# Attention and a feed-forward block on one Trainium2 core: GpSimd's shifted additions as 64-bit integer adds with the addend in the instruction

## The chip, the cores and the metric

The kernel runs on one core of a Trainium2 chip. The metric is the device time of one execution in microseconds. Beside TensorE (PE in the profile, its weight loads PEld) a core has VectorE (DVE), ScalarE (ACT), GpSimd (POOL) and SyncE (SP, which here issues DMAs). All have queues of their own and wait for each other by semaphores.

## The reference

A layer norm of x, attention with 32 heads of size 20 that share one key and one value head, and a feed-forward block with silu, all added up; 2048 positions of width 640:

```python
x = A_x
xn = _layernorm(x, axis=-1)
# A: q = xn @ wq (32 heads), k = xn @ wk, v = xn @ wv (one head)
scores = jnp.einsum("bhqd,bkd->bhqk", q, k) * (Dh ** -0.5)
p = _softmax(scores, axis=-1)
o = jnp.einsum("bhqk,bkd->bhqd", p, v)
# B: h = silu(xn @ w1); out = h @ w2
return x + o_merged @ wo + B
```

## The kernel before

The scores are made transposed: a block is 128 keys by 512 queries of one head. There are 2048 blocks (32 heads, 4 chunks of queries, 16 tiles of keys), in 32 groups of 64 (four heads of one chunk). PE makes the scores of a block in a bank of PSUM (the matmuls of L1122). From there a block goes one of two ways.

- On ACT, `exp` (L1156), two or three blocks in an instruction, into the ring `E`.
- On VectorE, without an exponential: the score is scaled so that its value, clamped and written as a 16-bit integer (L1171, into `Z`), has the bits of a bfloat16 that approximates the exponential. One such reading is coarse. Two more readings of the same numbers, shifted by 43 and by 86 (`PH`), are written into `Y`, and the three are multiplied with three differently scaled copies of v and added up by PE.

These shifted additions are the work that the change touches. `flush_z` is called when up to three blocks (`ZB`) have been gathered in one of four sets (`NZ`) of `Z` and `Y`. It makes two additions for each set. The second always goes to GpSimd (L1208); the first goes to GpSimd or VectorE (L1202), whichever the planner thinks will be free earlier. On GpSimd the 16-bit numbers are taken in pairs as 32-bit integers, and what is added is a tensor: one word for each partition, with the constant twice in it (`cy`, set at L1594), broadcast along the row.

PE then multiplies the readings with v (the PV matmuls, L962), adding up a whole group in one bank. At a group's end VectorE copies the bank out (L1252), a DMA transposes it, VectorE takes the reciprocal of the sums (L1236), and GpSimd multiplies (L1241, a tensor_tensor, `normalise`; the last group does this on VectorE). So GpSimd's queue has, in each group, about a dozen additions and one multiplication. At the start it also does a part of the layer norm, and makes the second copy of the keys (L1805, a tensor_scalar), of which VectorE's blocks have need.

The projections, the feed-forward block and the output's matmuls (most of L861) are filled in between by PE; VectorE and ACT take their results out.

The order of everything is set before the run by a planner (`Sched`): each operation has a supposed duration, the planner plays the engines through, and what it commits is the order of each engine's queue, with semaphore waits for each dependence. For an addition on GpSimd it reckons `YP_FIX + YP_BLK * n`, that is 0.15 + 0.426 n us for n blocks. An operation with `lock` isn't planned beside a locked one of the other of VectorE and GpSimd, and a GpSimd operation also waits for the last VectorE addition planned before it. In the run no queue changes its order.

Of the kernel before, what the change touches and what calls it, by code (L numbers as in the profile page):

```python
# [9 lines left out]
F32 = mybir.dt.float32  # L10
I16 = mybir.dt.int16
I32 = mybir.dt.int32
AF = mybir.ActivationFunctionType
ALU = mybir.AluOpType

# [33 lines left out]
PH = ((0, 1.0), (43, 0.8046875), (86, 0.625))  # L49
# [387 lines left out]
def t_dve_4x(n):  # L437
    return n / 3840.0 + 0.065
# [10 lines left out]
def t_act(n):  # L449
    return n / 1200.0 + 0.0635  # L450
# [27 lines left out]
class Builder:  # L478
# [16 lines left out]
    def sb(self, shape, dt):  # L495
        self.nsb += 1
        return self.stack.enter_context(self.nc.sbuf_tensor(f"sbt{self.nsb}", shape, dt))

    def alloc(self):
# [40 lines left out]
        self.eps = sb([P, 1], F32)  # L540
        self.cy = sb([P, 2], I32)
        self.zero = sb([P, 512], BF16)
# [526 lines left out]
    def do_S(self, now):  # L1069
# [76 lines left out]
        for run in runs:  # L1146
# [7 lines left out]
            def efn(a, run=run, na=na, b0=b0, step=step):  # L1154
                src = self.ps[:, :].rearrange("p (b n) -> p b n", n=BANK)[:, run[0]:run[-1] + 1:step, :]
                return a.activation(self.E[:, b0 * QW:(b0 + na) * QW].rearrange("p (b n) -> p b n", n=QW), src, AF.Exp,  # L1156
                                    scale=ACT_SCALE)
# [29 lines left out]
    def flush_z(self):  # L1187
        sc = self.sc
        zs = self.zset
        n = len(self.zblocks)  # L1190
        self.zset = (self.zset + 1) % NZ
        zk = [("Z", zs, i) for i in range(n)]
        w = n * QW
        back = {e: max(sc.t[e], sc.t["pe"]) + sum(o.dur for o in sc.pend[e]) for e in ("dve", "pool")}
        tp = YP_FIX + YP_BLK * n
        td = Y_SLOW + t_dve_4x(w)
        y0 = "pool" if back["pool"] + tp * Y0_COST < back["dve"] + td + Y0_POOL else "dve"
        self.y0_pool += y0 == "pool"
        for k, e in ((0, y0), (1, "pool")):
            yk = [("Y", zs, k, i) for i in range(n)]  # L1200
            if e == "dve":
                sc.new("dve", td, lambda v, k=k: v.tensor_scalar(  # L1202
                    self.Y[:, zs, k, 0:w], self.Z[:, zs, 0:w], float(PH[k + 1][0]), None, ALU.add), zk, yk,
                    prio=4.0, name=f"y{k}").lock = True
                continue
            c = self.cy[:, k:k + 1]
            cb = bass.AP(self.cy, c.offset, [list(c.ap[0]), [0, w // 2]])
            sc.new("pool", tp, lambda v, k=k, cb=cb: v.tensor_tensor(  # L1208
                self.Y[:, zs, k, 0:w].bitcast(I32), self.Z[:, zs, 0:w].bitcast(I32), cb, ALU.add), zk + [("cy",)], yk,
                prio=4.0, name=f"yp{k}").lock = True  # L1210
        for i, (t, g, kt, j) in enumerate(self.zblocks):
            for k in range(2):
                self.item(g, j, kt, k + 1, lambda k=k, i=i: self.Y[:, zs, k, i * QW:(i + 1) * QW].bitcast(BF16),
                          [("Y", zs, k, i)])
            self.g_late[g] -= 1
        self.zblocks = []
# [50 lines left out]
    def q_job(self, ht, act=False, lo=0, hi=QW):  # L1267
# [7 lines left out]
        def consume(b):  # L1275
# [3 lines left out]
            if act:  # L1279
                sc.new("act", t_act(hi - lo), lambda a: a.activation(dst, self.bk(b, 0, hi - lo), AF.Identity, bias=self.offq[:, :],  # L1280
                                                                scale=C1), [("B", b), ("offq",)], ks, prio=2.0,
# [42 lines left out]
    def h_job(self, c, fk, step):  # L1324
# [17 lines left out]
        def consume(b):  # L1342
            tp = fk % 2
            t = self.tb[0:rows, tp, :]
            src = self.bk(b, 0, QW, 0, rows)
            sc.new("act", t_act(QW), lambda a: a.activation(t, src, AF.Tanh, scale=0.5), [("B", b)], [("tb", tp)],  # L1346
                   prio=TH_PRIO, name=f"th{c}_{fk}").late = 0.06
# [40 lines left out]
    def out_job(self, c, i, e, step=-1, ffn=True, ks=range(DC), src="xres", dst="ost", use=None):  # L1388
# [18 lines left out]
        def consume(b):  # L1407
# [22 lines left out]
            if src == "ps":  # L1430
                sc.new("act", t_act(320), lambda a: a.activation(ost[:, e0:e0 + 320], ps, AF.Copy, scale=0.5),  # L1431
                       [("B", b)], wk, prio=X_PRIO, name=f"out{n}_{e}")
# [93 lines left out]
    def prologue(self):  # L1526
# [92 lines left out]
        def wkrep(a):  # L1619
            dst = self.wk[:, :, :].rearrange("p c (r j) -> p c r j", j=SLOT)[:, :, :, 0:DH]  # L1620
            s = self.kv_st[:, 0, :, :]
            src = bass.AP(self.U, s.offset, [list(s.ap[0]), list(s.ap[1]), [0, 4], [1, DH]])
            return a.activation(dst, src, AF.Copy)
        np_("act", t_act(400), wkrep, [("st", "k")], [("wk",)], prio=1.0, name="wkrep")
        for kk in range(2):
            np_("act", t_act(400), lambda a, kk=kk: a.activation(wqd[:, :, 4 * kk:4 * kk + 4, 0:DH],
                                                                 wqs[:, :, 4 * kk:4 * kk + 4, :], AF.Copy),
                [("wqd", kk)], [("wq", kk)], prio=1.0 + 5 * kk, name=f"wq{kk}")
# [28 lines left out]
        def mvk(a, b_):  # L1657
            return [("mv", n) for n in range(a, b_)]
# [30 lines left out]
        def newton(a, b_, pr, eng):  # L1689
# [5 lines left out]
            def nw(fn, r, w):  # L1695
                ch.append(np_(eng, 0.09, fn, r, w, prio=pr, name="nw"))
                ch[-1].lock = True
                self.last_nw = ch[-1]
                if len(ch) > 1:
                    ch[-2].then = ch[-1]  # L1700
            nw(lambda v: v.tensor_scalar(v_, self.mv[:, a:b_, 1], EPS, None, ALU.add), mvk(a, b_), [("va", a)])
            nw(lambda v: v.tensor_scalar(y_.bitcast(I32), v_.bitcast(I32), -0.5, 1597463007.0, ALU.mult, ALU.add),
               [("va", a)], [("rs", a)])
# [199 lines left out]
```

## Time and profile before

| | before |
|---|---|
| median of 3 runs | 672.74 us (672.58 to 672.9) |
| the profiled execution | 672.72 us |
| its span, first to last instruction | 670.8 us |
| busy: PE, ACT, DVE, POOL | 662.6, 657.7, 621.4, 570.3 us |
| additions on GpSimd (L1208) | 373, 529.9 us busy |
| additions on VectorE (L1202) | 107, 61.5 us busy |
| GpSimd's multiplications (L1241) | 31, 22.6 us busy |

The times come from one profiled execution, beside which the others were measured without a profile. A line of a view names the source line, the engine, the operation, and what it writes and reads (partitions x elements and type). "Idle before, releaser" is how long the engine had nothing to do in front of these instructions, and what ended that. PE's ends are modelled; the other engines' are seen.

### The profile page before, as it was taken

Reading aid. Unit: us, or ns where it says so; the run is one execution under the profiler, and the core shown is the slowest. Engines: PE = TensorE matmul, PEld = TensorE weight load, DVE = VectorE, ACT = ScalarE, POOL = GpSimd, SP = SyncE. Lnnn points to the kernel's source line nnn. Section 1 sums busy time; section 2 is a strip of 40 time slices with the busy share of each in tenths; the row PEclk is TensorE's granted clock in tenths of the full one; section 3 lists DMA queues with packets and bytes.
Section 4 is the critical chain, followed back from the end, with each engine's and each line's share of the span. In section 5 each row is a group of like instructions: output and inputs, shape, how many; then the busy total and the mean of one; then the engine's idle time right before and its main releaser. Section 6 shows DMA issues by size and latency. Waiting matters only on the chain.

```text
span 670.8 us, 22772 instructions
## 1 busy us (share of the span) xinstructions
PE 662.6 (99%) x9713; PEld 223.7 (33%) x9715; DVE 621.4 (93%) x1099; ACT 657.7 (98%) x730; POOL 570.3 (85%) x475
## 2 busy tenths in 40 slices
PE   8999999999999999999999999999999999999998
PEld 4422223333333233333333333332222333333224
DVE  7889999998999998999999999999999999999995
ACT  7999999999999999999999999999999999999995
POOL 6799987598989997789989888878989888888783
PEclk9999999999999999999999999999999999999999
DMA  7568000000013100010003210000000320000101
GB/s 209 96 229 251 25 15 12 10 10 18 10 23 103 29 10 18 10 11 17 18 1 50 84 30 11 10 10 18 17 10 10 79 66 10 11 17 11 33 9 41
DMA packets 51385, 27.72 MB, mean 41 GB/s; under 512 B 37238, under 2 KB 50646, under 8 KB 51286
## 3 DMA queue, kind: packets, MB, share of 16 engines
q1 hardware_dynamic: 49830, 26.05, 14.6%
q8 instruction: 78, 1.28, 0.8%
q10 hardware_dynamic: 1456, 0.22, 0.2%
q14 instruction: 21, 0.17, 0.1%
HBM read 11.44 MB, written 2.62 MB: 21 GB/s over the span
## 4 chain that ended last, share of the span: by engine, by line
PE 85%; ACT 8%; DVE 3%; POOL 2%; DMA 1%; SPq 1%; issue 0%; DVEq 0%; POOLq 0%
PE psall L962 30%; PE psall L1122 28%; PE psall L861 26%; ACT sbt L1156 8%; DVE sbt L1171 1%; DVE sbt L1682 1%; DVE sbt L1652 1%; DMA sbt<-in_A_x_dram 1%; SPq L1542 0%; POOL sbt L1208 0%; POOL sbt L1678 0%; DMA sbt<-sbt 0%; PE psall L1336 0%; POOL sbt L1805 0%; PE psall L828 0%
## 5 line engine op out<-in xcount | busy, mean ns | idle before, releaser
L1156 ACT ACTIVATE sbt<-psall 128x1024 bf16<-128x1024 f32 (+1 forms) x638 | 624.7, 1133 | 2.1 <-PE psall L1122 1.5
L1208 POOL TENSOR_TENSOR sbt<-sbt 128x768 int32<-128x768 int32 (+1 forms) x373 | 529.9, 1449 | 75.9 <-DVE sbt L1202 58.1
L1171 DVE TENSOR_SCALAR sbt<-psall 128x512 int16<-128x512 f32 x707 | 463.5, 685 | 34.0 <-PE psall L1122 23.0
L962 PE MATMUL psall<-sbt 128*32 128x512 bf16 x3462 | 265.4, 383 | 0.0
L1122 PE MATMUL psall<-sbt 32*128 32x512 bf16 x2048 | 248.9, 384 | 1.7 <-DVE sbt L1422 0.5
L861 PE MATMUL psall<-sbt 128*32 128x320 bf16 (+2 forms) x3939 | 225.9, 331 | 0.4 <-DVE sbt L1654 0.3
L1122 PEld LDWEIGHTS psall<-sbt 32*128 32x128 bf16 x2048 | 64.3, 91 | 241.4 <-issue 87.0
L861 PEld LDWEIGHTS psall<-sbt 128*32 128x32 bf16 x3939 | 83.8, 95 | 87.1 <-issue 53.7
L962 PEld LDWEIGHTS psall<-sbt 128*32 128x32 bf16 x3462 | 65.4, 95 | 98.3 <-issue 70.0
L1202 DVE TENSOR_SCALAR sbt<-sbt 128x1536 int16<-128x1536 int16 (+2 forms) x107 | 61.5, 588 | 0.1
L1351 DVE SCALAR_TENSOR_TENSOR sbt<-sbt,psall 128x512 bf16<-128x512 bf16 x54 | 36.7, 679 | 0.8 <-ACT sbt L1346 0.5
L1346 ACT ACTIVATE sbt<-psall 128x512 bf16<-128x512 f32 x54 | 36.2, 670 | 0.0
L1241 POOL TENSOR_TENSOR sbt<-sbt 128x320 bf16<-128x320 bf16 x31 | 22.6, 729 | 4.3 <-DVE sbt L1202 3.4
L1252 DVE CAST sbt<-psall 128x512 bf16<-128x512 f32 x32 | 21.8, 682 | 2.6 <-PE psall L962 2.4
L1415 DVE SCALAR_TENSOR_TENSOR sbt<-psall,sbt 128x320 bf16<-128x320 f32 x28 | 13.6, 484 | 0.9 <-PE psall L861 0.7
L1434 DVE SCALAR_TENSOR_TENSOR sbt<-psall,sbt 128x320 bf16<-128x320 f32 x28 | 13.2, 482 | 1.0 <-PE psall L861 1.0
L1303 DVE TENSOR_SCALAR sbt<-psall 128x512 bf16<-128x512 f32 (+1 forms) x19 | 13.0, 683 | 1.1 <-PE psall L861 1.0
L837 PE MATMUL psall<-sbt 128*128 128x512 bf16 (+3 forms) x43 | 11.9, 424 | 1.3 <-DVE sbt L1591 1.2
L1652 DVE BATCH_NORM_STATS2 sbt<-sbt 128x6 f32<-128x320 bf16 x20 | 9.0, 472 | 3.2 <-DMA sbt<-in_A_x_dram 3.0
L1236 DVE RECIPROCAL sbt<-sbt 128x16 f32<-128x16 bf16 x31 | 7.6, 244 | 0.0
L837 PEld LDWEIGHTS psall<-sbt 128*128 128x128 bf16 x45 | 4.6, 107 | 6.6 <-issue 2.4
L1431 ACT ACTIVATE sbt<-psall 128x320 bf16<-128x320 f32 x4 | 1.6, 438 | 4.3 <-PE psall L861 4.2
(70 smaller groups left out, 93.8 us busy)
## 6 DMA issues: line engine op xcount, KB each, us to landing
sbt<-in_A_x_dram SPq DMA_DIRECT2D x32, 160.0 KB, 3.5
out_dram<-sbt SPq DMA_DIRECT2D x15, 160.0 KB, 2.0
sbt<-in_B_w_dram SPq DMA_DIRECT2D x5, 432.0 KB, 6.0
sbt<-sbt SPq DMA_DIRECT2D x105, 20.0 KB
sbt<-in_B_w_dram SPq DMA_DIRECT2D x13, 160.0 KB, 3.0
sbt<-sbt SPq DMA_DIRECT2D x1, 1024.0 KB, 6.1
sbt<-sbt SPq DMA_TRANSPOSE x56, 2.4
sbt<-in_A_wo_dram SPq DMA_DIRECT2D x5, 160.0 KB, 2.8
```

Of the source, the lines that this page charges most:

```text
L837: return pe.matmul(self.bk(b, 0, n), self.zero[:, 0:P], self.zero[:, 0:n], start=True, stop=True)
L861: ins = pe.matmul(self.bk(b, 0, n, r, r + SLOT), w[:, r:r + SLOT], x, start=start, stop=stop, tile_position=(0, r), skip_group_check=True)
L962: ins = pe.matmul(self.bk(ub[k], 0, QW, r, r + SLOT), self.v[:, it.w, it.kt, :], it.x(), start=f, stop=False, tile_position=(0, r), skip_g ...
L1122: ins = pe.matmul(self.bk(bank[x]), self.kT[r:r + SLOT, kk, kt * P:(kt + 1) * P], self.qT[r:r + SLOT, g % 8, (g // 8) % 2, :], start=True, ...
L1156: return a.activation(self.E[:, b0 * QW:(b0 + na) * QW].rearrange("p (b n) -> p b n", n=QW), src, AF.Exp, scale=ACT_SCALE)
L1171: return v.tensor_scalar(self.Z[:, zs, zp * QW:(zp + 1) * QW], self.bk(bb), 0.0, ZMAX, ALU.max, ALU.min)
L1202: sc.new("dve", td, lambda v, k=k: v.tensor_scalar(self.Y[:, zs, k, 0:w], self.Z[:, zs, 0:w], float(PH[k + 1][0]), None, ALU.add), zk, yk, ...
L1208: sc.new("pool", tp, lambda v, k=k, cb=cb: v.tensor_tensor(self.Y[:, zs, k, 0:w].bitcast(I32), self.Z[:, zs, 0:w].bitcast(I32), cb, ALU.ad ...
L1241: op = sc.new(eng, 0.69 if eng == "pool" else t_dve_ps(16 * DH), lambda v: v.tensor_tensor(dst, ut[:, :, :, 0:DH], rb, ALU.mult), [key, (" ...
L1252: sc.new("dve", t_dve_ps(QW), lambda v: v.tensor_copy(self.U[:, up, :], self.bk(ub)), [("B", ub)], [("U", up)], prio=U_PRIO, name=f"Uev{g}")
L1346: sc.new("act", t_act(QW), lambda a: a.activation(t, src, AF.Tanh, scale=0.5), [("B", b)], [("tb", tp)], prio=TH_PRIO, name=f"th{c}_{fk}") ...
L1351: sc.new("dve", t_dve_ps(QW), lambda v: v.scalar_tensor_tensor(out=self.hT[0:rows, fk, :], in0=t, scalar=1.0, in1=src, op0=ALU.add, op1=AL ...
```

## The change

The GpSimd additions are issued as `int64_add` in place of `tensor_tensor`. The same 16-bit numbers are taken four at a time as one 64-bit integer, and the addend is a number in the instruction (the constant four times), not a tensor. No sum goes over 16 bits, so nothing is carried from one number into the next. The planner's durations and all dependences stay (that on `cy` too, though it isn't read any more), so each queue has its operations in the same order as before.

```diff
+I64 = mybir.dt.int64
...
-            c = self.cy[:, k:k + 1]
-            cb = bass.AP(self.cy, c.offset, [list(c.ap[0]), [0, w // 2]])
-            sc.new("pool", tp, lambda v, k=k, cb=cb: v.tensor_tensor(
-                self.Y[:, zs, k, 0:w].bitcast(I32), self.Z[:, zs, 0:w].bitcast(I32), cb, ALU.add), zk + [("cy",)], yk,
+            c = PH[k + 1][0] * (1 + (1 << 16) + (1 << 32) + (1 << 48))
+            sc.new("pool", tp, lambda v, k=k, c=c: v.int64_add(
+                self.Y[:, zs, k, 0:w].bitcast(I64), self.Z[:, zs, 0:w].bitcast(I64), c), zk + [("cy",)], yk,
                 prio=4.0, name=f"yp{k}").lock = True
```

`int64_add` is an instruction of the program builder's own: `out = in0 + in1` over 64-bit words, exact. The builder has a table of which set of GpSimd code holds which instruction. Its stock set lists tensor_tensor, tensor_scalar and others; the sets that list `int64_add` list neither of these two.

## The prediction

> **What bounds the kernel now.** I read the page's head and chain first, then the busy times by stretch, the groups by form, the waits, and GpSimd's own timeline.
>
> ```profile
> span 670.8 us, 22772 instructions
> PE 662.6 (99%) x9713; PEld 223.7 (33%) x9715; DVE 621.4 (93%) x1099; ACT 657.7 (98%) x730; POOL 570.3 (85%) x475
> PE 85%; ACT 8%; DVE 3%; POOL 2%; DMA 1%; SPq 1%; issue 0%; DVEq 0%; POOLq 0%
> L1156 ACT ACTIVATE sbt<-psall 128x1024 bf16<-128x1024 f32 (+1 forms) x638 | 624.7, 1133 | 2.1 <-PE psall L1122 1.5
> ```
>
> Two engines are full, PE (its ends are modelled) and ACT (its ends are seen). ACT runs the exponentials of L1156 and waited only 2.1 us in front of all 638 of them. GpSimd is the one engine with air, 15%, and has 2% of the chain. The stretch that carries the attention, from the first normalisation to the last, says it more sharply:
>
> ```profile
> core 0: us, PE busy (x) PEld busy (x) DVE busy (x) ACT busy (x) POOL busy (x), PEclk, DMA share, GB/s
> 58.30:653.00 594.70, 593.39 (x8832) 194.12 (x8820) 560.93 (x956) 593.87 (x645) 517.31 (x381) 1.00 0.11 28
> ```
>
> ACT is busy for 593.87 of 594.70 us, so GpSimd's speed as such is worth almost nothing here. POOL is idle for 594.70 - 517.31 = 77.4 us. Who waits for whom:
>
> ```profile
> POOL sbt L1208 <- DVE sbt L1202: 58.1, 72, 2.1
> POOL sbt L1208 <- DVE sbt L1171: 17.0, 19, 1.8
> PEld psall L962 <- POOL sbt L1208: 5.5, 24, 0.3
> DVE sbt L1171 <- POOL sbt L1208: 0.7, 3, 0.2
> ```
>
> The adds of L1208 wait for VectorE, for 75 us in all, and are waited for by the PV matmuls of L962, 24 times, at most 0.3 us each. PE runs a fixed order, so these 24 places say that the plan brings many shifted readings only just in time. A late add stops PE at once, and with PE, soon after, ACT.
>
> **The change, the add itself.** 373 adds change form. What they cost now, and the nearest one-input rows:
>
> ```profile
> L1208 POOL TENSOR_TENSOR sbt<-sbt 128x768 int32<-128x768 int32 x360 | 517.8, 1467 | 71.7 <-DVE sbt L1202 54.0 <-DVE sbt L1171 17.0
> L1208 POOL TENSOR_TENSOR sbt<-sbt 128x256 int32<-128x256 int32 x2 | 1.2, 612 | 0.8 <-DVE sbt L1202 0.8
> L1678 POOL TENSOR_SCALAR sbt<-sbt 128x640 bf16<-128x640 bf16 x3 | 2.6, 879 | 0.0
> L1805 POOL TENSOR_SCALAR sbt<-sbt 128x256 bf16<-128x256 bf16 x8 | 3.8, 482 | 0.5 <-DVE sbt L1803 0.5
> L1241 POOL TENSOR_TENSOR sbt<-sbt 128x320 bf16<-128x320 bf16 x31 | 22.6, 729 | 4.3 <-DVE sbt L1202 3.4 <-DVE sbt L1236 0.9
> ```
>
> With two inputs an element costs (1467 - 612) / 512 = 1.67 ns. With one input it costs (879 - 482) / 384 = 1.03 ns over a fixed 217 ns. The new add has one input, since the addend is in the instruction. Of 1536 readings it makes 384 words of 64 bits: if each is one step, 217 + 384 x 1.03 = 614 ns; if each goes as two 32-bit halves, 217 + 768 x 1.03 = 1011 ns. I take the middle, 0.81 us, and keep 0.61 and, as if nothing were won, 1.47 as ends. At 0.81 an add saves 0.66 us, and all of them 373 x 0.66 = 246 us of GpSimd's time. By the waits above that buys PE 5.5 us of waits at the most, and the end only what ACT lost, 2.1 us.
>
> **The change, what has to be loaded.** No row shows this; it is read from the program's text. The 64-bit add isn't one of GpSimd's stock instructions. The builder's table puts it into a set of GpSimd code that is loaded at run time and that holds neither the tensor_tensor of L1241 nor the tensor_scalar of L1805, and the stock set doesn't hold the 64-bit add. Where the resident set may lack an instruction, the builder puts a load in front of it, on GpSimd's own queue. Today's adds share a set with L1241 and L1805; after the change each alternation is a load. How often they alternate:
>
> ```profile
> 27.28 1.47 POOL L1208 TENSOR_TENSOR sbt<-sbt 128x768 int32<-128x768 int32 x1
> 28.73 0.48 POOL L1805 TENSOR_SCALAR sbt<-sbt 128x256 bf16<-128x256 bf16 x1
> 29.17 1.47 POOL L1208 TENSOR_TENSOR sbt<-sbt 128x768 int32<-128x768 int32 x1
> 30.62 0.94 POOL L1805 TENSOR_SCALAR sbt<-sbt 128x256 bf16<-128x256 bf16 x2
> 31.52 1.47 POOL L1208 TENSOR_TENSOR sbt<-sbt 128x768 int32<-128x768 int32 x1
> 32.96 0.48 POOL L1805 TENSOR_SCALAR sbt<-sbt 128x256 bf16<-128x256 bf16 x1
> 33.41 1.47 POOL L1208 TENSOR_TENSOR sbt<-sbt 128x768 int32<-128x768 int32 x1
> 35.42 0.48 POOL L1805 TENSOR_SCALAR sbt<-sbt 128x256 bf16<-128x256 bf16 x1 [0.54 <-DVE sbt L1803]
> 35.87 12.85 POOL L1208 TENSOR_TENSOR sbt<-sbt 128x768 int32<-128x768 int32 x9
> 48.66 0.63 POOL L1765 MEMSET sbt<- 128x640 bf16 x1
> 49.79 8.58 POOL L1208 TENSOR_TENSOR sbt<-sbt 128x768 int32<-128x768 int32 x6 [0.50 <-DVE sbt L1202]
> 58.33 0.73 POOL L1241 TENSOR_TENSOR sbt<-sbt 128x320 bf16<-128x320 bf16 x1
> ```
>
> Up to 58.33 us that is one load ahead of the first add and two for each of four excursions to L1805: 9 (a plain memset needs no set). After that L1241 comes 31 times, each time with adds before and behind it, the last time too:
>
> ```profile
> L1241 POOL TENSOR_TENSOR sbt<-sbt x31: 724/729/734, 58.3 to 653.0; 128x320 bf16<-128x320 bf16 x31
> L1208 POOL TENSOR_TENSOR sbt<-sbt x373: 612/1466/1475, 27.3 to 660.3; 128x768 int32<-128x768 int32 x180, 128x512 int32<-128x512 int32 x5, 128x256 int32<-128x256 int32 x2
> ```
>
> So 62 more, 71 in all. A last one that restores the stock set comes after 661 us and has about 9 us to the end of the span: I cost it at nothing; with that cover gone it is one load.
>
> The price of a load isn't in the trace. The nearest rows are a table load on ACT and transfers by size:
>
> ```profile
> L1727 ACT ACT_TABLE_LOAD x1 | 1.3, 1283 | 1.8 <-issue 1.8
> ```
> ```profile
> sbt<-in_B_w_dram SPq DMA_DIRECT2D x5, 432.0 KB, 6.0
> sbt<-in_B_w_dram SPq DMA_DIRECT2D x13, 160.0 KB, 3.0
> sbt<-sbt SPq DMA_DIRECT2D x1, 1024.0 KB, 6.1
> ```
>
> Code for eight cores is nearer to a large transfer than to one table, and GpSimd must come to rest and start again around it, about the 0.50 us that a hand-over takes it at 49.79. I take 6.1 + 0.5 = 6.6 us. The ends are 1.3 (the table) and 12 (two transfers of 6.0, if fetching and first use come one after the other). The Trainium skill's GPSIMD Engine Reference, Instruction dispatch, says that the first call of a freshly loaded kernel also pays an instruction-memory load of about 6 us (5.95 measured), not visible as an instruction; by that figure alone the sum below would be 984 us, and no run here has shown it yet.
>
> **The sum.** The start, 27.28 to 58.33: 9 x 6.6 = 59.4 us of loads; 19 adds save 12.5, and 0.54 + 0.50 us of idle time can go: 45.9 us late. The adds and the key copies there feed PE directly, so this is all lost. The main stretch: around each L1241 GpSimd stands still for 2 x 6.6 = 13.2 us more than now. Against that it has its idle time, 77.4 / 31 = 2.5 us per normalisation, and 0.66 us from the faster first add: 10.04 us late, for the first add behind it. The adds after that run faster than PE asks for them (11.4 per normalisation, 9.2 us of work in about 20), so the delay comes once per normalisation: 31 x 10.04 = 311.2 us. Queued behind a load are the adds; PE waits for these, and ACT and VectorE for PE's scores. The lateness doesn't carry over, because the next normalisation is put off with the rest.
>
> The profiled execution took 672.72 us, 1.92 more than its span, and stands 0.02 below the median of the runs. 672.72 + 45.9 + 311.2 = 1029.8, say 1030 us. The add's own ends move this little: at 0.61 us it is 10 less; at 1.47, 33 more.
>
> **Rivals.**
>
> *PE runs at half speed after each standstill (1083 us, 25%).* The kernel's first matmuls, which wait for nothing, show such a phase:
>
> ```profile
> core 0: us, PE busy (x) PEld busy (x), PEclk, DMA share, GB/s
> 1.10:4.50 3.40, 3.31 (x8) 1.16 (x9) 1.00 0.79 178
> 4.50:9.20 4.70, 4.70 (x22) 2.11 (x21) 1.00 0.98 297
> ```
>
> Eight in 3.40 us, then 22 in 4.70: 425 ns each against 214, while the granted clock reads 1.00 in both. Half of 3.40 us is lost, 1.7; if each of 31 standstills of 10 us brings it back, 31 x 1.7 = 53 us more. Against it: ACT sets the pace, and PE has waits to give up. The Trainium skill's TensorE: Matmul & The Clock Gate, Part 1, has this rule: idle for about 3.4 us, half the clock until about 3.4 us of work; the start agrees, and before this change no later stretch can show it.
>
> *GpSimd only has to be fast enough on average (836 us, 10%).* If lateness is absorbed by the four sets of buffers, only GpSimd's own work counts: 71 x 6.6 + 373 x 0.81 + 31 x 0.73 + 6 x 0.48 + 0.63 = 797 us from 27.3 on, 9.4 us of tail and the 1.92. For it: four sets exist. Against it: PE already waits 24 times.
>
> *Loads at other prices.* At 3.0 us (the 160 KB row) 31 x (6.0 - 3.16) + 27 - 13.5 = 101 us are added: 774 us, 6%. At 12 us, 31 x 20.84 + 94.5 = 740: 1413 us, 5%.
>
> *Faster (670.6 us, 3%), or no change (6%).* If the code is resident after all, or a load is short, only the lighter add is left. The place is the idle time around L1241: two loads fit into 2.5 + 0.66 = 3.16 us, so the point is 1.58 us a load (at the start 13.5 / 9 = 1.5). Below that, PE's 5.5 us of waits go and ACT gets at most its 2.1 us back. The table load's 1.3 us speaks for it, the transfer rows against it.
>
> **How the numbers follow.** The forecast itself has 45%: 1030 us. Left out of the range are the cheap loads, the very dear ones, and the two cases of no loss, 20% together. 830 takes in the absorbed case. Loads of 9 us make 672.72 + 31 x 14.84 + 67.5 = 1200, and with the slow phase 1253: the upper end is 1250. Slower: 45 + 25 + 10 + 6 + 5 = 91%. About 0.2%, 1.35 us, is what can be told from no change here; within it 6%, faster 3%.
>
> **What would show it.** Right: adds of about 0.8 us; in front of each L1241 and of the first add behind it, 6 to 7 us in which GpSimd does nothing that VectorE explains, 62 times; L962's waits for L1208 up from 5.5 to about 300 us; ACT with as much idle time, busy about 64%; a first such pause before 30 us. The slow phase would show as eight or so matmuls at twice their spacing behind each pause. Wrong: no pauses, or pauses only once; adds over 1.5 us; ACT still full.

## The result and the profile after

| | before | after |
|---|---|---|
| median of 3 runs | 672.74 us | 1091.01 us (1086.82 to 1097.08) |
| ratio | 1 | 1.6227, 95% interval 1.6104 to 1.635 |
| the profiled execution, its span | 672.72, 670.8 us | 1086.82, 1084.9 us |
| additions on GpSimd, mean of one | 1449 ns | 813 ns |

The additions became 44% shorter, and the kernel takes 62% longer. The page's head, its row of granted clocks and its chain, after:

```profile
span 1084.9 us, 22914 instructions
PE 738.9 (68%) x9713; PEld 230.2 (21%) x9715; DVE 623.8 (57%) x1099; ACT 671.5 (62%) x730; POOL 341.7 (31%) x475
PEclk8755888788789888878888879888888888888888
PE 58%; issue 26%; DVE 8%; POOL 6%; ACT 2%; DMA 0%; DVEq 0%; POOLq 0%
```

No engine is full any more, and 26% of the chain is "issue", time in which an engine waited for nothing that the profile shows. The groups and the waits name the engine:

```profile
L1157 ACT ACTIVATE sbt<-psall 128x1024 bf16<-128x1024 f32 (+1 forms) x638 | 637.0, 1096 | 394.6 <-PE psall L1123 393.3
L1208 POOL INT64_ADD sbt<-sbt x373 | 299.6, 813 | 461.6 <-issue 208.2
L1241 POOL TENSOR_TENSOR sbt<-sbt 128x320 bf16<-128x320 bf16 x31 | 22.2, 717 | 220.3 <-issue 112.8
```
```profile
ACT sbt L1157 <- PE psall L1123: 393.3, 111, 15.2
PE psall L963 <- POOL sbt L1208: 305.2, 40, 13.5
POOL sbt L1208 <- issue: 208.2, 35, 6.3
POOL sbt L1241 <- issue: 112.8, 16, 7.8
POOL sbt L1241 <- DVE sbt L1172: 100.5, 14, 7.7
```

ACT waits for PE's scores, PE for GpSimd's additions (305.2 us; before only its weight loads did, 5.5 us), and GpSimd, ahead of these, for nothing. "Issue" means 208.2 / 35 = 5.95 us in front of an addition and 112.8 / 16 = 7.05 in front of a normalisation. Of the other pauses in front of L1241, 14 are put down to VectorE's L1172; they are as long (100.5 / 14 = 7.2), so the name only says which semaphore came last. GpSimd's timeline shows both kinds (start, duration, instruction, pause ahead of it):

```profile
8.99 0.28 POOL L1587 TENSOR_SCALAR_AFFINE_SELECT sbt<-sbt 128x128 f32<-128x128 f32 x1 [8.00 <-issue]
...
41.22 0.82 POOL L1208 INT64_ADD sbt<-sbt  x1 [5.95 <-issue]
51.25 0.47 POOL L1805 TENSOR_SCALAR sbt<-sbt 128x256 bf16<-128x256 bf16 x1 [9.22 <-issue]
57.64 0.82 POOL L1208 INT64_ADD sbt<-sbt  x1 [5.92 <-issue]
...
127.22 0.72 POOL L1241 TENSOR_TENSOR sbt<-sbt 128x320 bf16<-128x320 bf16 x1 [7.83 <-issue]
133.82 2.42 POOL L1208 INT64_ADD sbt<-sbt  x3 [5.89 <-issue]
...
1061.23 0.72 POOL L1241 TENSOR_TENSOR sbt<-sbt 128x320 bf16<-128x320 bf16 x1 [6.78 <-issue]
1067.77 2.42 POOL L1208 INT64_ADD sbt<-sbt  x3 [5.82 <-issue]
```

In GpSimd's queue each of these pauses begins with a pair of short instructions that the views by line count (least, median and largest duration in ns, then the first and the last start; the row of the additions is shown with them):

```profile
L1241 POOLq MODIFY_POOL_CONFIG  x62: 10/11/13, 119.4 to 1054.5; - x62
...
L1208 POOL INT64_ADD sbt<-sbt x373: 387/824/829, 41.2 to 1072.9; - x187
L1208 POOLq MODIFY_POOL_CONFIG  x72: 1/1/11, 35.5 to 1062.2; - x72
...
L1805 POOLq MODIFY_POOL_CONFIG  x8: 1/1/1, 42.1 to 87.6; - x8
...
L1587 POOLq MODIFY_POOL_CONFIG  x2: 11/11/11, 1.1 to 1.2; - x2
```

Ahead of L1241, L1208 and L1805 that makes 31, 36 and 4 pairs: 71 loads. One more pair stands ahead of L1587, the program's first stock instruction. The kernel before has that pair too, at the same place, and there the pause is 0.17 us:

```profile
L1587 POOLq MODIFY_POOL_CONFIG  x2: 11/11/11, 1.1 to 1.1; - x2
...
1.18 0.29 POOL L1587 TENSOR_SCALAR_AFFINE_SELECT sbt<-sbt 128x128 f32<-128x128 f32 x1 [0.17 <-POOL sbt L1594]
```

So a pair alone doesn't stop the engine; what the 8.00 us of the changed kernel hang on is shown by the last experiments. Over the 31 normalisations the pause ahead of L1241 is 7.10 us in the mean (6.73 to 7.83), and that ahead of the first addition behind it 5.94 (5.76 to 6.28).

The 414.1 us by which the span grew lie in three places. The first L1241 moved from 58.33 to 127.22 us: 68.9 more. From there to the last one it was 594.7 us and is 934.0: 339.3 more, 11.3 for each of 30 intervals. Behind the last it was 17.8 us and is 23.7: 5.9 more, the load ahead of 1067.77.

### The profile page after: what moved, and what is told of

Its sections match the earlier page's. It is cut to its first block, busy times and chain, and to the rows that moved or that the text cites. A ratio compares the mean times of both kernels' runs of the same rounds, so it can differ in the third digit from the quotient of the medians.

```text
span 1084.9 us, 22914 instructions
## 1 busy us (share of the span) xinstructions
PE 738.9 (68%) x9713; PEld 230.2 (21%) x9715; DVE 623.8 (57%) x1099; ACT 671.5 (62%) x730; POOL 341.7 (31%) x475
## 2 busy tenths in 40 slices
DMA packets 51386, 27.73 MB, mean 26 GB/s; under 512 B 37238, under 2 KB 50646, under 8 KB 51286
## 4 chain that ended last, share of the span: by engine, by line
PE 58%; issue 26%; DVE 8%; POOL 6%; ACT 2%; DMA 0%; DVEq 0%; POOLq 0%
PE psall L963 21%; PE psall L1123 18%; PE psall L862 17%; DVE sbt L1172 6%; POOL sbt L1208 3%; POOL sbt L1241 2%; ACT sbt L1157 2%; DVE sbt L1203 0%; PE psall L1795 0%; DVE sbt L1303 0%; PE psall L1776 0%; DMA sbt<-sbt 0%; DVE sbt L1351 0%; PE psall L1336 0%; PE psall L1815 0%
## 5 line engine op out<-in xcount | busy, mean ns | idle before, releaser
L1157 ACT ACTIVATE sbt<-psall 128x1024 bf16<-128x1024 f32 (+1 forms) x638 | 637.0, 1096 | 394.6 <-PE psall L1123 393.3
L1172 DVE TENSOR_SCALAR sbt<-psall 128x512 int16<-128x512 f32 x707 | 467.1, 685 | 428.5 <-PE psall L1123 388.8
L963 PE MATMUL psall<-sbt 128*32 128x512 bf16 x3462 | 309.2, 433 | 305.2 <-POOL sbt L1208 305.2
L1208 POOL INT64_ADD sbt<-sbt x373 | 299.6, 813 | 461.6 <-issue 208.2
L1123 PE MATMUL psall<-sbt 32*128 32x512 bf16 x2048 | 269.5, 418 | 24.7 <-POOL sbt L1805 12.3
L862 PE MATMUL psall<-sbt 128*32 128x320 bf16 (+2 forms) x3939 | 236.2, 343 | 0.1
L963 PEld LDWEIGHTS psall<-sbt 128*32 128x32 bf16 x3462 | 68.7, 98 | 430.1 <-POOL sbt L1208 329.3
L862 PEld LDWEIGHTS psall<-sbt 128*32 128x32 bf16 x3939 | 86.3, 98 | 95.7 <-issue 63.2
L1241 POOL TENSOR_TENSOR sbt<-sbt 128x320 bf16<-128x320 bf16 x31 | 22.2, 717 | 220.3 <-issue 112.8
L1203 DVE TENSOR_SCALAR sbt<-sbt 128x1536 int16<-128x1536 int16 (+2 forms) x107 | 56.9, 545 | 0.1
L1415 DVE SCALAR_TENSOR_TENSOR sbt<-psall,sbt 128x320 bf16<-128x320 f32 x28 | 13.5, 484 | 1.2 <-PE psall L862 1.0
L1434 DVE SCALAR_TENSOR_TENSOR sbt<-psall,sbt 128x320 bf16<-128x320 f32 x28 | 13.2, 482 | 1.4 <-PE psall L862 1.4
L1805 POOL TENSOR_SCALAR sbt<-sbt 128x256 bf16<-128x256 bf16 x8 | 3.8, 470 | 30.6 <-issue 30.6
L1776 PE MATMUL psall<-sbt 128*128 128x128 bf16 x35 | 4.0, 260 | 7.8 <-DVE sbt L1682 7.7
```

The source lines that it names most:

```text
L862: ins = pe.matmul(self.bk(b, 0, n, r, r + SLOT), w[:, r:r + SLOT], x, start=start, stop=stop, tile_position=(0, r), skip_group_check=True)
L963: ins = pe.matmul(self.bk(ub[k], 0, QW, r, r + SLOT), self.v[:, it.w, it.kt, :], it.x(), start=f, stop=False, tile_position=(0, r), skip_g ...
L1123: ins = pe.matmul(self.bk(bank[x]), self.kT[r:r + SLOT, kk, kt * P:(kt + 1) * P], self.qT[r:r + SLOT, g % 8, (g // 8) % 2, :], start=True, ...
L1172: return v.tensor_scalar(self.Z[:, zs, zp * QW:(zp + 1) * QW], self.bk(bb), 0.0, ZMAX, ALU.max, ALU.min)
L1203: sc.new("dve", td, lambda v, k=k: v.tensor_scalar(self.Y[:, zs, k, 0:w], self.Z[:, zs, 0:w], float(PH[k + 1][0]), None, ALU.add), zk, yk, ...
L1208: sc.new("pool", tp, lambda v, k=k, c=c: v.int64_add(self.Y[:, zs, k, 0:w].bitcast(I64), self.Z[:, zs, 0:w].bitcast(I64), c), zk + [("cy", ...
```

## The experiments

**Loads or additions?** The first kernel keeps the 32-bit additions of before and has the loads: behind each of GpSimd's 31 normalisations stands a 64-bit addition of two 32-bit words.

```diff
             ins = v.tensor_tensor(dst, ut[:, :, :, 0:DH], rb, ALU.mult)
+            if eng == "pool":
+                v.int64_add(self.lz[:, 2:4].bitcast(I64), self.lz[:, 0:2].bitcast(I64), 1)
```

> The kernel before with its 32-bit adds; behind each of the 31 GpSimd normalisations a tiny 64-bit add of two words is issued, so that the code sets alternate there as in the changed kernel (two loads each, and one at the program's start), but not at the key copies. If the loads are the cost: 31 standstills of 13.0 us less the 2.5 us of idle time, about 325 us, with up to 1 us more each for a slow clock, and 8 us at the start: 1005 to 1040 us. If the 64-bit add itself or its way to memory is the cost: 31 tiny adds, 673 to 682 us.

Measured: 1103.01 us, ratio 1.6377 (1.6328 to 1.6425). No data of the result goes through a 64-bit addition, and the whole loss is there. GpSimd's timeline of this kernel (L1247 is the small addition, L1245 the normalisation, L1211 the 32-bit additions):

```profile
134.31 0.18 POOL L1247 INT64_ADD sbt<-sbt  x1 [5.88 <-issue]
141.60 8.14 POOL L1211 TENSOR_TENSOR sbt<-sbt 128x768 int32<-128x768 int32 x6 [7.11 <-issue]
```

The time is 63 us above the expected range. From the first L1245 to the last it is 1070.3 - 59.0 = 1011.3 us, or 13.9 for each interval more than before, where the changed kernel loses 11.3. My reading, not shown by a run of its own: six additions that have piled up take 8.14 us here, where the 64-bit ones would take about 4.9, so nothing of a load is won back.

The second kernel is the other half: the changed kernel's 64-bit additions and almost no alternation. GpSimd's normalisations and key copies are plain copies, for which the builder puts in no load.

```diff
-        op = sc.new(eng, 0.69 if eng == "pool" else t_dve_ps(16 * DH), lambda v: v.tensor_tensor(
-            dst, ut[:, :, :, 0:DH], rb, ALU.mult), [key, ("rL", up)], [("o", h0 + i) for i in range(4)],
+        def nrm_fn(v):
+            if eng == "pool":
+                return v.tensor_copy(dst, ut[:, :, :, 0:DH])
+            return v.tensor_tensor(dst, ut[:, :, :, 0:DH], rb, ALU.mult)
...
-                sc.new("pool", K1_COST, lambda g: g.tensor_scalar(d1, dst, self.offk[:, :], 1.0, ALU.add, ALU.mult), ...
+                sc.new("pool", K1_COST, lambda g: g.tensor_copy(d1, dst), ...
```

> The changed kernel with all 373 64-bit adds, but GpSimd's normalisations and key copies are plain copies, which need no code set (left out: the division by the sums on GpSimd, and the keys' offset). Two loads are left on the way, one at the program's start and one ahead of the first add. If the loads are the cost: 672.7 + 8 + about 6, 680 to 690 us. If the adds are: near 1090 us. If the lighter add were worth something by itself: under 672 us.

Measured: 687.86 us, ratio 1.0228 (1.0213 to 1.0243). Its head, and the row of its copies of L1243, which stand where the normalisations stood:

```profile
PE 668.1 (97%) x9713; PEld 225.1 (33%) x9715; DVE 617.6 (90%) x1099; ACT 658.2 (96%) x730; POOL 333.0 (49%) x475
...
L1243 POOL COPY sbt<-sbt x31: 449/450/452, 72.2 to 668.0; 128x320 bf16<-128x320 bf16 x31
```

From the first to the last copy it is 595.8 us, against 594.7 before: GpSimd is busy half the time in place of 85%, and nothing is won. What is lost lies ahead of 72.2 us, in two pauses of 7.72 us (affine_select) and 5.98 us (first addition).

**Once for each normalisation?** In the third kernel every second group has the plain copy, the others the division.

```diff
+            if eng == "pool" and g % 2:
+                return v.tensor_copy(dst, ut[:, :, :, 0:DH])
```

> The changed kernel with the normalisations of odd groups as plain copies (left out: the division there): 16 of 31 normalisations keep their two loads; those at the key copies stay. If each standstill is lost in full (11.3 us each, as the changed kernel shows): 1091 - 15 x 11.3 = 920 us. If only GpSimd's average load counts: 10.0 us of adds, 0.7 and 6.5 us of loads in each group of 19.8 us fit, so the main stretch loses nothing and about 760 us remain.

Measured: 919.88 us, ratio 1.3664 (1.3642 to 1.3687). 15 pairs of loads taken away gain 1091.0 - 919.9 = 171.1 us, 11.4 for each; PE's waits fall by nearly half:

```profile
PE psall L963 <- POOL sbt L1208: 166.9, 23, 13.0
```

So lateness is not averaged over the groups, and the rival by average load falls.

**The price of a load.** The fourth kernel has four loads for a normalisation in place of two.

```diff
             if eng == "pool":
+                v.int64_add(self.lz[:, 2:4].bitcast(I64), self.lz[:, 0:2].bitcast(I64), 1)
+                v.tensor_tensor(self.lt[:, 2:4], self.lt[:, 0:2], self.lt[:, 0:2], ALU.add)
```

> The changed kernel with one more alternation behind each of the 31 normalisations (a tiny 64-bit add of two words and a tiny 32-bit float add), so four loads in place of two. If a load is lost in full: two more of 7.1 + 5.95 = 13.0 us, 31 x 13.0 = 405 us: about 1495 us. If loads one behind the other overlap or are found in place: under 1300 us.

Measured: 1508.73 us, ratio 2.2422 (2.2359 to 2.2485). The additional 62 loads cost 417.7 us, 6.74 each, their two small instructions included. Four in a row on GpSimd's timeline:

```profile
175.47 0.72 POOL L1244 TENSOR_TENSOR sbt<-sbt 128x320 bf16<-128x320 bf16 x1 [6.70 <-issue]
181.99 0.18 POOL L1246 INT64_ADD sbt<-sbt  x1 [5.80 <-issue]
188.87 0.18 POOL L1247 TENSOR_TENSOR sbt<-sbt 128x2 f32<-128x2 f32 x1 [6.70 <-issue]
194.94 4.12 POOL L1210 INT64_ADD sbt<-sbt  x5 [5.89 <-issue]
```

Behind the first pair nothing is hidden any more.

**Is it the standstill alone, and how much of it is hidden?** Two kernels take the one without alternation and put a standstill of known length ahead of each copy: 5 or 22 memsets in a chain, each waiting for the one before.

```diff
             if eng == "pool":
+                for _ in range(5):          # 22 in the other
+                    if self.n_still:
+                        v.wait_ge(self.s_still, self.n_still)
+                    v.memset(self.sp_[:, :], 0.0).then_inc(self.s_still, 1)
+                    self.n_still += 1
                 return v.tensor_copy(dst, ut[:, :, :, 0:DH])
```

> The kernel without alternations (688 us; it leaves out the division by the sums on GpSimd and the keys' offset) with 5 memsets of 448 columns in a chain ahead of each of the 31 normalisations, 2.5 to 3 us in which GpSimd is only kept. If a group can hide 3.16 us: 688 us, within 3. If each late add stops PE at once: 31 x 2.5, about 765 us.

> As the run with 5 memsets, with 22 (11 to 13 us). If a load costs by nothing else than the time for which GpSimd stands still: for 13 us 688 + 31 x 10 to 11 = 1000 to 1030 us, for 11 us 62 less. If a load also disturbs others (memory, DMAs): well under 950 us.

Measured: 699.43 us, ratio 1.0399 (1.0382 to 1.0416), and 1019.79 us, ratio 1.5155 (1.5132 to 1.5178). A chain of the shorter kernel and one of the longer:

```profile
113.59 2.59 POOL L1249 MEMSET sbt<- 128x448 bf16 x5
...
103.33 11.58 POOL L1249 MEMSET sbt<- 128x448 bf16 x22
```

Both times are above what was expected for these lengths: 688 us for the shorter, and for the longer 963 to 993, between the figures for 11 and 13 us. Over the 31 chains the shorter standstill is 2.65 us in the mean (2.58 to 3.00). Against 687.86 it costs 11.6 / 31 = 0.37 us each, so some 2.3 us of it are hidden, and not the 3.16 expected. The longer is 11.8 us in the mean (11.57 to 12.48) and costs 331.9 / 31 = 10.7, so 1.1 us are hidden, or 1.8 to 2.7 if the slower clock that follows (granted 0.836 here) adds 0.7 to 1.6, as below. An engine that merely stands still makes nearly the loss of the loads: 10.7 us for 11.8, where the loads make 11.4 for 13.05.

**What is the slow clock worth?** PE, ACT and GpSimd around one standstill of the changed kernel:

```profile
190.10 0.61 PE L963 MATMUL psall<-sbt 128*32 128x512 bf16 x8
193.66 0.72 POOL L1241 TENSOR_TENSOR sbt<-sbt 128x320 bf16<-128x320 bf16 x1 [6.96 <-issue]
200.38 2.42 POOL L1208 INT64_ADD sbt<-sbt  x3 [6.01 <-issue]
201.25 0.62 PE L963 MATMUL psall<-sbt 128*32 128x512 bf16 x4 [10.54 <-POOL sbt L1208]
202.35 1.04 PE L963 MATMUL psall<-sbt 128*32 128x512 bf16 x8
202.47 1.02 ACT L1157 ACTIVATE sbt<-psall 128x1024 bf16<-128x1024 f32 x1 [11.00 <-PE psall L1123]
```

Eight matmuls take 1.04 us behind the pause and took 0.61 ahead of it. To take this away, matmuls with zeros, which add nothing, were put on PE's queue between its own work and the wait for the first addition behind a normalisation: 30, and in another kernel 48.

```diff
+            def warm(eng, b=op.ub0):          # ahead of the waits of that PV step
+                for _ in range(NWARM):
+                    eng.matmul(self.bk(b, 0, QW, 0, SLOT), self.zero[:, 0:SLOT], self.zero[:, 0:QW], start=False, ...
```

> The changed kernel; ahead of the first PV matmul that waits behind each of the 31 normalisations PE is given 30 matmuls of zeros (6.4 us at full speed), which run while it would stand still. If the slow clock after a standstill is part of the cost: the granted clock rises from 0.81, and 31 x 1.7 = 53 us go: about 1040 us. If it isn't, since ACT sets the pace: 1085 to 1097 us as before.

> As the run with 30 matmuls of zeros ahead of each waiting PV matmul, with 48 (10.2 us at full speed, about the whole standstill of 10.5 to 11 us; with 30 PE still stood still for the last 4 us and came back at half speed). If the slow clock is part of the cost: the matmuls behind the standstill run at their usual spacing, the granted clock is near 1, and 31 x 1.0 to 1.7 us go from 1091: 1038 to 1060 us. If ACT sets the pace: no better than the 1073 us with 30.

Measured: 1072.98 us (1.5946, 1.5903 to 1.5989) and 1068.51 us (1.588, 1.5856 to 1.5904). PE behind the same standstill with 30 and then with 48:

```profile
203.04 0.62 PE L987 MATMUL psall<-sbt 128*32 128x512 bf16 x4 [4.35 <-POOL sbt L1233]
...
204.13 1.05 PE L987 MATMUL psall<-sbt 128*32 128x512 bf16 x8
```
```profile
191.24 10.52 PE L514 MATMUL psall<-sbt 128*32 128x512 bf16 x48
202.39 0.40 PE L987 MATMUL psall<-sbt 128*32 128x512 bf16 x4 [0.63 <-POOL sbt L1233]
...
203.05 0.62 PE L987 MATMUL psall<-sbt 128*32 128x512 bf16 x8
```

With 30 PE still idles 4.35 us here and is slow again, as behind 14 of the 31 standstills. With 48 the matmuls keep their pace, and the time falls by 1091.0 - 1068.5 = 22.5 us, 0.73 for each standstill. That is less than the 31 to 53 expected, and it is the least that the slow phase can be worth, since the zeros cost time themselves: where a standstill would have been shorter than 48 matmuls, PE is still busy with zeros when the addition is done. One such place, with 48:

```profile
717.03 10.10 PE L514 MATMUL psall<-sbt 128*32 128x512 bf16 x46
723.06 3.60 POOL L1233 INT64_ADD sbt<-sbt  x5 [6.14 <-issue]
726.76 0.40 PE L987 MATMUL psall<-sbt 128*32 128x512 bf16 x3
```

The first of the five additions is done at 723.9, and PE's own matmul starts 2.9 us later. The trace has this at 17 of the 31 places, 26.7 us in all. If all of that reached the end, the slow phase would be worth 22.5 + 26.7 = 49 us, 1.6 for each standstill. So it makes 5 to 12% of the loss; where in between, no run here shows.

**The pause at the program's start.** The changed kernel and that without alternation stand still for 8.00 and 7.72 us at their first stock instruction. The one with loads alone, whose last GpSimd instructions are stock additions, doesn't. So the kernel without alternation was given one more instruction behind its last addition.

```diff
         def with_stock(v):                    # the last operation on GpSimd's queue
             ins = add(v)
+            v.tensor_tensor(self.lt[:, 2:4], self.lt[:, 0:2], self.lt[:, 0:2], ALU.add)
             return ins
```

> The kernel without alternation (normalisations and key copies as plain copies, so division and key offset are left out), with one more instruction: behind GpSimd's last 64-bit addition a tensor_tensor of two elements, so that GpSimd's last code is the stock set's. Without it the run took 687.86 us, its first stock instruction (the affine_select) stood still 7.72 us, and the last addition lies about 9 us before the end. Theory: the pause at the program's start is the load that goes back to the stock set, put off by the execution before to this one's first stock instruction; the kernel with loads alone, which ends on stock additions, had no such pause (its affine_select started at 1.42 us). Then the affine_select starts at about 1.4 us, and as the load at the end lies in the tail, 7 to 8 us are saved: about 680 us. Rival: a program that uses another set always loads at its start, or a restore at the end is made in any case and clears nothing: the affine_select still starts at 8.7 us and the time stays at 687 to 690.

Measured: 679.52 us, ratio 1.0097 (1.008 to 1.0113), 8.3 us less than without it.

```profile
1.42 0.29 POOL L1599 TENSOR_SCALAR_AFFINE_SELECT sbt<-sbt 128x128 f32<-128x128 f32 x1 [0.43 <-POOL sbt L1606]
...
674.27 0.18 POOL L500 TENSOR_TENSOR sbt<-sbt 128x2 f32<-128x2 f32 x1 [7.32 <-issue]
```

The load has moved from the start to the tail, where 7.32 us of standstill hold up nobody. The pair of the start is still there, ahead of L1599, but finds the stock set in place. What remains over before (673.28 us beside this kernel) is 6.2 us, about the one load ahead of the first addition (5.82).

**A whole version with one change of sets.** Last, a kernel that leaves nothing out, with the normalisations on VectorE and a new plan:

```diff
-        self.normalise(g, ut, ("UT", up), "pool")
+        self.normalise(g, ut, ("UT", up), "dve")
...
-        tp = YP_FIX + YP_BLK * n
+        early = self.nflush < EARLY
+        self.nflush += 1
+        tp = YP_FIX + YP_BLK * n if early else YP64_FIX + YP64_BLK * n
...
+            if not self.loaded:
+                self.loaded = True
+                tp += LOAD
```

`EARLY` is 3: the first three sets keep the 32-bit additions.

> A whole version that changes sets once and not 71 times. The first three sets of additions on GpSimd stay 32-bit, so that all key copies lie ahead of the first 64-bit addition; the normalisations go to VectorE (in the kernel before they take 22.6 us of GpSimd's busy time); a tensor_tensor of two elements behind the last addition goes back to the stock set in the tail. The planner is given 0.19 + 0.2066 us a block for a 64-bit addition and 6.0 us for the one load, and its preferences are searched anew, so the order of all queues is another. Its plan ends at 670.05 us, that of the kernel before at 668.08, which ran in 672.74. Theory (the alternation is the whole loss, the lighter addition gains next to nothing where ACT is full, and one load cannot be hidden at the start, which fed PE directly before too): 672.74 + 670.05 - 668.08 = 674.7, between 673 and 679; additions of about 0.82 us, POOL busy near 420 us, one pause of 6 us ahead of the first 64-bit addition and one of 7 us ahead of the last instruction, none in between. Rival: the lighter addition is worth something once VectorE and GpSimd are planned with it: below 672. Other rival: 64-bit additions cost PE something beside the loads (their stores or the loads' rest): above 682.

Measured: 677.61 us, ratio 1.0074 (1.0062 to 1.0087). Inside the expected range, 2.9 us above the 674.7 that followed from the plan; no version here beats the kernel before.

```profile
PE 665.5 (98%) x9740; PEld 224.4 (33%) x9740; DVE 602.2 (89%) x1046; ACT 654.2 (97%) x735; POOL 418.2 (62%) x561
...
PE 85%; DVE 6%; ACT 5%; POOL 2%; DMA 1%; issue 1%; SPq 0%; DVEq 0%; POOLq 0%
...
L1171 POOL INT64_ADD sbt<-sbt x482 | 389.5, 821 | 235.2 <-DVE sbt L1123 219.3 <-DVE sbt L1156 6.4 <-PE psall L1074 5.0
```

GpSimd makes 482 additions in the 64-bit form and is still busy for only 62%, and VectorE is relieved to 89%; PE and ACT are about as full as they were, and PE makes 85% of the chain, as before. The one load ahead of the 64-bit additions took 7.22 us, where 6 were expected. Whether another plan would come out some microseconds lower was not tested.

## Why the prediction was right, and where its sum was off

It said 1030 us, slower, and its mechanism held at every place that was tested. The terms:

- **What bounds the kernel.** ACT full, GpSimd's speed worth almost nothing: right. Without the alternation the main stretch takes 595.8 us against 594.7.
- **The addition.** 0.81 us predicted, 813 ns measured. That it fits is luck. The shortest additions, of one block, take 387 ns and those of three blocks 824, so a word of 64 bits costs (824 - 387) / 256 = 1.71 ns over a fixed 168 ns. The two readings between which the prediction took the middle were 1.03 and 2.06 ns over 217.
- **The number of loads.** 71 predicted and 71 found, but one more is paid: the step "a last one that restores the stock set", costed at nothing because it comes in the tail, failed. No pair stands behind the last addition. The set is changed back by the pair ahead of the next execution's first stock instruction, which every version here has, and there 8.00 us lie on the path. The kernel that ends on the stock set shows the place: 8.3 us went with that pause.
- **The price of a load.** 6.6 us predicted; 7.10 back to the stock set and 5.94 to the other, 6.5 in the mean. The number held, its reason is not shown, so that it held is luck as far as is known: the page's DMA rows count 27.73 MB after and 27.72 before, so these rows show no transfers for the loads. The Trainium skill's GPSIMD Engine Reference, Instruction dispatch, gives 5.95 us for the first call of a freshly loaded kernel, with no instruction to be seen. The trace agrees with it ahead of the 64-bit additions (5.94), but not on the way back (7.10), and not for the single load of the whole version (7.22).
- **The start.** 45.9 us predicted. 68.9 were measured up to the first L1241, of which 7.8 are that instruction's own load, so 61.1 compare. The nine loads took 60.4 (59.4 predicted) and the load at the start 8.0; of the 13.5 us that lighter additions and idle time were to give back, 7.3 came.
- **Each normalisation.** 10.04 us predicted for each of 31, 311.2 in all. Measured: 7.8 + 339.3 + 5.9 = 353.0, 11.4 each. The loads are right (13.05 us for 13.2). Of the 41.8 us that are missing, the slow clock, which the sum put at nothing, takes at least 22.5. The rest is open: the clock can have taken all of it, since it was worth up to 49; or less time was hidden than the 2.5 + 0.66 = 3.16 us that were reckoned. With 0.73 us for the clock 13.05 + 0.73 - 11.4 = 2.4 us of each pair were hidden, with 1.5 us the whole 3.16. The chains of memsets give 2.3 and 1.8 to 2.7, which speaks for somewhat less than 3.16. My reading, not shown: GpSimd's idle time is scattered over a group, and not all of it lies where a late start can use it.

The start's 15.2 us and these 41.8 make up the 57.0 between 357.1 us predicted and 414.1 measured in the profiled execution. (The 22.5 is a difference of two medians, and the median of the changed kernel lies 4.2 us above its profiled execution, so such shares are known to a few microseconds at best.)

The rivals. *PE at half speed*, 1083 us, is the nearest number, 8 us from the median, and its phase is real: the matmuls are slow behind all 31 standstills. It was reckoned at 53 us and is worth 22.5 to 49. With it the sum is 1052 to 1079 us, and the load at the start adds 8 more. So the rival's phase and the forecast's mechanism are both there, and how far its nearness is chance stays as open as that share. What the prediction reads beside the first matmuls, a granted clock of 1.00, is no measured value: the clock records of that trace begin at 4.83 us. The Trainium skill's TensorE: Matmul & The Clock Gate, Part 1, has half the clock after about 3.4 us of idling: the trace agrees on the kind (1.04 us for 0.61, and again after an idle time of 4.35 us). With 30 zeros, though, PE also came back slow after an idle time of 2.40 us (at 787.89) and at its pace after one of 3.60 (at 510.38).

*Average load*, 836 us, falls with the half loads (its sum counts six key copies, where the timeline has five behind the first addition: half a microsecond). *Faster or no change* fall with the 71 pauses; even with the alternation gone the kernels take 679.5 and 677.6 us.

Predicted for the profile and found: pauses of 6 to 7 us 62 times, waits of the PV matmuls for additions of about 300 us (305.2), ACT at about 64% (62%). A first pause ahead of 30 us was found too, but it is the affine_select's, and the one meant, ahead of the first addition, ended at 41.22.

## What to carry to other kernels

Before an instruction on GpSimd is exchanged for a faster one, look up which set of code it is in, and count how often the queue changes between sets: here each change stands the engine still for 5.9 to 7.1 us, as long as seven to nine of the new additions. Look also at what a program's last GpSimd instruction leaves resident, since the next execution pays for it at its start (8.00 us here). And an engine with air can be made 40% lighter without any gain, while of a standstill on it all that goes beyond its local slack (some 2 to 3 us here) comes through.

## What the runs showed of the hardware that was not expected

- A pair of MODIFY_POOL_CONFIG costs a load only where the set isn't already there. Ahead of its first stock instruction each program here has one: 8.00 us in a program that ended on the other set, 0.17 in the kernel before, 0.43 where the last instruction was a stock one.
- The two directions cost differently: 7.10 us (6.73 to 7.83) back to the stock set ahead of the normalisations, 5.94 (5.76 to 6.28) to the 64-bit one. Single loads took longer: 9.22 ahead of the first key copy, 7.22 to the 64-bit set in the whole version.
- The granted clock of the records falls with PE's idle times, to a mean of 0.814 in the changed kernel, 0.731 with doubled loads and 0.963 with PE kept busy by 48 matmuls.
